# Clustered attention and an ELU product pair on one core: scores computed transposed, with the products of a batch placed beside the next batch's attention

## The chip, the core and the metric

The program runs on one core of a Trainium2 chip. Five engines have queues of their own: TensorE (PE; PEld is its weight load), VectorE (DVE), ScalarE (ACT), GpSimd (POOL) and SyncE (SP, which here issues the transfers). The metric is the device time of one execution in microseconds, median over the runs. A change of about 1% either way is taken as the least that can be told from none.

## The reference

Inputs: `q`, `k`, `v` of 4 batches x 8 heads x 768 tokens x 64, `centroids` of 8 heads x 16 x 64, all float32; `w_in` 512 x 2048 and `w_out` 2048 x 512, which arrive as float64.

```
q_assign = argmax(q_n . c_n)      k_assign = argmax(k_n . c_n)      # 16 clusters for each head
scores   = (q . k^T) / 8, and -1e9 where q_assign != k_assign
attn     = softmax over the keys (maximum subtracted first)
x        = attn . v, heads side by side: 3072 tokens x 512
h        = x @ w_in;  g = h where h > 0, else exp(h) - 1;  out = g @ w_out
```

In the reference's own arrays every one of the 4 x 8 x 16 clusters has between 26 and 72 keys (counted from them).

## The kernel before

Sixteen units of work, `pairs`: a batch and two heads. Of a pair, `turn_head` transposes q and k to 64 rows x 768 tokens with TensorE (line 183); `assign` multiplies each 128 tokens with the 16 centroids (line 200: 24 products of only 16 columns, each with a weight load of its own) and makes one-hot rows on VectorE; `clusters` transposes these (line 228) and puts them below q and k as rows 64 to 79 (`aug`), so that one product over 80 rows gives the masked score. `prepare` runs this for the next pair while a pair is in work.

A score tile is 128 queries x 768 keys of one head (`softmax`, line 254). VectorE takes the maximum (264), ScalarE the exponential and the row sum (265), VectorE the reciprocal and the product with it (268 to 270). The keys then lie along the free dimension, but the product with v sums over keys, so `turn_probs` transposes each tile in six pieces on TensorE (281), and the results are copied out of PSUM by VectorE and ScalarE in turn (`evacuate`, lines 70 and 72). `values` (292) multiplies v, 64 columns for each head: the two heads go to the upper and lower 64 partitions of one PSUM tile. When the four pairs of a batch have half their tokens done, `mlp` runs both products for these 384 tokens: 64 products into `bank` (310) with the ELU on VectorE, ScalarE, VectorE (318, 319, 321), and 48 into `o` (327). Nothing else is written beside it.

The weights are turned from float64 words to float32 in 32 pieces of 128 x 512 (`convert`): six VectorE steps (146, 148, 151, 152, 153, 158) and two of GpSimd (147, 159) each, one piece beside each score tile from the start on.

Each float32 product appears in the trace as two MATMUL instructions (`mlp` asks for 512 products at line 310; the trace has 1024); a transpose appears as one. The emitted order isn't quite that of the code: the tile framework moves instructions.

Of the kernel before, what the change touches and what calls it, by code (L numbers as in the profile page):

```python
# [11 lines left out]
U32 = mybir.dt.uint32  # L12
Act = mybir.ActivationFunctionType
# [4 lines left out]
P = 128  # L18
# Added to the score of a query and a key of different clusters. It is a power of two, so
# the products with the one-hot rows are exact, and so large that a score disappears in it:  # L20
# a query whose cluster has no key gets equal scores for all keys.
BIG = float(2.0**80)


@with_exitstack
def kernel(
# [11 lines left out]
    ctx.enter_context(nc.allow_non_contiguous_dma(reason="token and weight layouts"))  # L38

    B, H, S, D = q.shape  # L40
# [8 lines left out]
    FG = NT  # L49
    KA = D + NC  # L50
    SCALE = 1.0 / 8.0
    assert D == 64 and NC == 16 and H * NC == P and S % (2 * P) == 0 and DM == H * D

    const = ctx.enter_context(tc.tile_pool(name="const", bufs=1))
    loads = ctx.enter_context(tc.tile_pool(name="loads", bufs=2))
    work = ctx.enter_context(tc.tile_pool(name="work", bufs=3))
    small = ctx.enter_context(tc.tile_pool(name="small", bufs=4))
    augp = ctx.enter_context(tc.tile_pool(name="augp", bufs=8))
    turned = ctx.enter_context(tc.tile_pool(name="turned", bufs=5))
    xtp = ctx.enter_context(tc.tile_pool(name="xtp", bufs=10))  # L60
    ps_s = ctx.enter_context(tc.tile_pool(name="ps_s", bufs=2, space=PSUM))
    ps_t = ctx.enter_context(tc.tile_pool(name="ps_t", bufs=2, space=PSUM))
    ps_o = ctx.enter_context(tc.tile_pool(name="ps_o", bufs=2, space=PSUM))

    turn = [0]

    def evacuate(out_, in_):
        turn[0] += 1
        if turn[0] % 2:
            nc.vector.tensor_copy(out_, in_)  # L70
        else:
            nc.scalar.copy(out_, in_)  # L72

    def bank(dtype=F32):
        t = ps_t.tile([P, 512], F32, name="bank", tag="t")
        return t if dtype == F32 else t.bitcast(dtype)

# [4 lines left out]
    def load(i):  # L82
        b, pr = pairs[i]
        for name, src, bufs in (("q", q, 2), ("k", k, 2), ("v", v, 3)):
            t = loads.tile([P, 2, NT, D], F32, name=f"{name}_raw", tag=name, bufs=bufs)
            nc.sync.dma_start(
                t.rearrange("p h t d -> p h (t d)"),
                src[b, 2 * pr : 2 * pr + 2].rearrange("h (p t) d -> p h (t d)", t=NT),
            )
            raw[name, i] = t  # L90

    cen = const.tile([P, D], F32, name="cen")
    nc.scalar.dma_start(cen, centroids.rearrange("h c d -> (h c) d"))
    load(0)

    ident = const.tile([P, P], F32, name="ident")
    make_identity(nc, ident)
    identb = const.tile([P, P], BF16, name="identb")
    nc.vector.tensor_copy(identb, ident)
    rev = const.tile([P, NC], F32, name="rev")  # L100
    nc.gpsimd.iota(
        rev, pattern=[[-1, NC]], base=NC, channel_multiplier=0, allow_small_or_imprecise_dtypes=True
    )

# [4 lines left out]
    cT = const.tile([D, P], F32, name="cT")  # L109
# [3 lines left out]
    # The square root, then one step of Newton's method.  # L113
# [6 lines left out]
    nc.vector.tensor_scalar(cen, cen, norm, None, op0=Alu.mult)  # L120
    cps = bank()
    nc.tensor.transpose(cps[:D, :P], cen, ident)
    nc.vector.tensor_copy(cT, cps[:D, :P])

# [1 line left out]
    # They come as float64, as words of 64 bits, and are rounded to float32 here. With the  # L126
    # low word and the high word (sign, 11 bits of exponent, 20 of mantissa) of a number,
    #     +-2^(exponent - 1023) * ((1 + mantissa / 2^20) + low / 2^52),
    # where the last sum rounds to the nearest. What float32 cannot hold becomes 0 or
    # infinity, as its exponent is held between 0 and 255.  # L130
    w_in = const.tile([P, KC, DF], F32, name="w_in")
    w_out = const.tile([P, FC, DM], F32, name="w_out")
# [3 lines left out]
    def convert(to, src):  # L136
        """The two steps of a piece; the first makes exponent and sign, the second the number."""
# [3 lines left out]
        ex = loads.tile([P, WC], U32, name="ex", tag="ex", bufs=2)  # L141
        low, high, bits = words[:, :, 0], words[:, :, 1], to.bitcast(U32)

        def begin():
            nc.sync.dma_start(words.rearrange("p n w -> p (n w)"), src.bitcast(U32))
# [17 lines left out]
    def weights():  # L163
        for g in range(DF // WC):
            for c in range(KC):
                yield w_in[:, c, ts(g, WC)], moe_w_in[ts(c, P), ts(g, WC)]
        for f in range(FC):
            yield w_out[:, f], moe_w_out[ts(f, P)]

# [103 lines left out]
    def turn_probs(i, half, hp, t):  # L273
        p = probs.pop((i, half, hp, t))
        if t == 0:
            probsT[i, half, hp] = turned.tile([P, NT, HS], F32, name="probsT", tag="turned")
# [139 lines left out]
```

## Time and profile before

| | us |
|---|---|
| median of 3 runs | 1575.28 |
| lowest, highest | 1571.52, 1582.56 |
| the profiled execution's span | 1583.6 |
| TensorE busy in it | 1524.0 (96%) |
| VectorE, ScalarE, GpSimd busy | 788.6, 406.2, 67.6 |

The profiled execution is 0.5% above the median, within 0.1% of the slowest of the runs. Matmuls are pipelined and the ends of their intervals are modelled: neighbours overlap. So a group's mean duration is longer than the distance from one start to the next, and its busy time divided by its count is nearer to that distance.

### The profile page before, as it was taken

The numbers are of one execution on the slowest core, as the hardware profiler recorded it, in microseconds if no ns is written. First come the engines' busy times: TensorE is split into PE (matmuls) and PEld (weight loads), VectorE is DVE, ScalarE is ACT, GpSimd is POOL, SyncE is SP. The second block draws the span as 40 slices with busy tenths as digits, with TensorE's granted clock in tenths as the row PEclk, the third lists the DMA queues.
The fourth block names the chain that finished last, engine by engine and source line by source line (L and its number), as shares of the span: only waits on it lengthen the run. The fifth ranks groups of instructions, "written<-read, shape, count | busy, mean of one in ns | idle before, by whom it ended". The sixth has DMA issues, their size and how long they took to land.

```text
span 1583.6 us, 15284 instructions
## 1 busy us (share of the span) xinstructions
PE 1524.0 (96%) x6017; PEld 883.5 (56%) x6017; DVE 788.6 (50%) x1623; ACT 406.2 (26%) x831; POOL 67.6 (4%) x71
## 2 busy tenths in 40 slices
PE   6888889999999999999999999999999999999999
PEld 4645446654555666654554666565554665654453
DVE  4879796540522665741431666742340567651230
ACT  1222222310311343420311333511210335331110
POOL 1223231000000000000000000000000000000000
PEclk6667766899999898999999898999999889899999
DMA  4223130100001001100000011000000000000000
GB/s 143 74 69 121 56 121 13 31 0 14 17 0 40 8 23 31 31 0 14 17 1 20 20 31 31 30 0 7 14 11 13 27 11 1 1 0 7 14 1 20
DMA packets 21336, 42.96 MB, mean 27 GB/s; under 512 B 1808, under 2 KB 14096, under 8 KB 21264
## 3 DMA queue, kind: packets, MB, share of 16 engines
q1 hardware_dynamic: 21120, 41.95, 8.2%
q8 instruction: 47, 0.77, 0.2%
q14 instruction: 25, 0.20, 0.0%
q10 hardware_dynamic: 144, 0.03, 0.0%
HBM read 35.68 MB, written 6.29 MB: 27 GB/s over the span
## 4 chain that ended last, share of the span: by engine, by line
PE 90%; DVE 5%; ACT 3%; issue 1%; DMA 1%; SPq 0%
PE bank L310 21%; PE o L327 21%; PE scores L254 16%; PE bank L281 10%; PE o L292 10%; PE bank L200 8%; PE bank L183 2%; ACT probs L265 2%; PE bank L228 2%; DVE probs L270 1%; DVE low L264 1%; DVE ex L148 1%; ACT aug L237 1%; DMA words<-in_moe_w_in_dram 1%; DVE probsT L70 0%
## 5 line engine op out<-in xcount | busy, mean ns | idle before, releaser
L254 PE MATMUL scores<-aug 80*128 80x384 f32 x768 | 344.3, 563 | 8.3 <-ACT probs L265 6.6
L310 PE MATMUL bank<-xT,w_in 128*128 128x384 f32 x1024 | 332.4, 487 | 0.0
L327 PE MATMUL o<-w_out,gT 128*128 128x512 f32 x768 | 330.9, 592 | 0.0
L310 PEld LDWEIGHTS bank<-xT,w_in 128*128 128x128 f32 x1024 | 193.9, 190 | 138.3 <-issue 4.8
L327 PEld LDWEIGHTS o<-w_out,gT 128*128 128x128 f32 x768 | 145.9, 190 | 182.0 <-issue 177.9
L281 PEld LDWEIGHTS bank<-ident,probs 128*128 128x128 f32 x1152 | 153.6, 159 | 136.9 <-issue 49.0
L281 PE MATMUL bank<-ident,probs 128*128 128x128 f32 x1152 | 204.9, 311 | 24.5 <-ACT probsT L72 10.8
L264 DVE TENSOR_REDUCE low<-scores 128x1 f32<-128x768 f32 x192 | 182.6, 951 | 28.1 <-PE scores L254 26.0
L72 ACT COPY probsT<-bank 128x384 f32<-128x384 f32 x192 | 91.9, 479 | 397.2 <-PE bank L281 396.4
L254 PEld LDWEIGHTS scores<-aug 80*128 80x128 f32 x768 | 143.1, 216 | 81.0 <-ACT probs L265 36.6
L265 ACT ACTIVATE probs<-scores,low 128x768 f32<-128x768 f32 x192 | 173.3, 902 | 35.9 <-DVE low L264 28.9
L292 PE MATMUL o<-probsT,v_raw 128*64 128x384 f32 x768 | 175.0, 524 | 0.3 <-DVE probsT L70 0.3
L70 DVE COPY probsT<-bank 128x384 f32<-128x384 f32 x192 | 104.9, 551 | 136.0 <-PE bank L281 135.5
L319 ACT ACTIVATE elu<-elu 128x384 f32<-128x384 f32 x128 | 66.9, 523 | 296.3 <-DVE elu L318 296.3
L200 PE MATMUL bank<-cT,aug 64*128 64x16 f32 x768 | 128.5, 317 | 4.1 <-DVE aug L190 4.1
L200 PEld LDWEIGHTS bank<-cT,aug 64*128 64x128 f32 x768 | 126.8, 260 | 9.9 <-DVE aug L190 4.3
L318 DVE TENSOR_SCALAR elu<-bank 128x384 f32<-128x384 f32 x128 | 71.4, 558 | 116.9 <-PE bank L310 116.9
L270 DVE TENSOR_SCALAR probs<-probs,den 128x768 f32<-128x768 f32 x192 | 124.2, 647 | 3.5
L321 DVE SCALAR_TENSOR_TENSOR gT<-elu,bank 128x384 f32<-128x384 f32 x128 | 71.0, 554 | 82.2 <-ACT elu L319 82.2
L70 DVE COPY o_sb<-o 128x512 f32<-128x512 f32 x8 | 5.5, 692 | 205.6 <-PE o L327 205.6
L292 PEld LDWEIGHTS o<-probsT,v_raw 128*64 128x64 f32 x768 | 59.5, 144 | 74.2 <-issue 70.1
L72 ACT COPY o_sb<-o 128x512 f32<-128x512 f32 x16 | 9.4, 586 | 315.5 <-PE o L327 315.5
(55 smaller groups left out, 626.6 us busy)
## 6 DMA issues: line engine op xcount, KB each, us to landing
words<-in_moe_w_in_dram SPq DMA_DIRECT2D x16, 512.0 KB, 3.9
words<-in_moe_w_out_dram SPq DMA_DIRECT2D x16, 512.0 KB, 3.5
q_raw<-in_q_dram SPq DMA_DIRECT2D x16, 384.0 KB, 3.1
k_raw<-in_k_dram SPq DMA_DIRECT2D x16, 384.0 KB, 3.9
v_raw<-in_v_dram SPq DMA_DIRECT2D x16, 384.0 KB, 3.1
out_dram<-o_sb SPq DMA_DIRECT2D x24, 256.0 KB, 2.0
cen<-in_centroids_dram ACTq DMA_DIRECT2D x1, 32.0 KB, 2.4
```

Source lines behind the costliest of these rows:

```text
L70: nc.vector.tensor_copy(out_, in_)
L72: nc.scalar.copy(out_, in_)
L200: nc.tensor.matmul(ps[:, (2 * hp + j) * NT + t], lhsT=aug[i, hp, j][:D, ts(t, P)], rhs=cT[:, ts(h, NC)], start=True, stop=True,)
L254: nc.tensor.matmul(s[:, ch, :HS], lhsT=aug[i, hp, 0][:, ts(half * HT + t, P)], rhs=aug[i, hp, 1][:, ts(ch, HS)], start=True, stop=True,)
L264: nc.vector.tensor_reduce(low, s[:, :, :HS], axis=Axis.XY, op=Alu.max, negate=True)
L265: nc.scalar.activation(p.rearrange("p (a b) -> p a b", a=2), s[:, :, :HS], Act.Exp, bias=low, accum_out=den)
L270: nc.vector.tensor_scalar(p, p, den, None, op0=Alu.mult)
L281: nc.tensor.transpose(ps[:, ts(kt, P)], p[:, ts(g * HT + kt, P)], ident)
L292: nc.tensor.matmul(o[D * hp : D * hp + D, :HS], lhsT=raw["v", i][:, hp, kt], rhs=probsT[i, half, hp][:, kt], start=(kt == 0), stop=(kt == ...
L310: nc.tensor.matmul(h, lhsT=w_in[:, c, ts(f, P)], rhs=xT[b, half, c], start=(c == 0), stop=(c == KC - 1),)
L318: nc.vector.tensor_scalar(e, h, 0.0, None, op0=Alu.min)
L327: nc.tensor.matmul(o, lhsT=g[f // FG][:, f % FG, ts(t, P)], rhs=w_out[:, f], start=(f == 0), stop=(f == FC - 1),)
```

## The change

The program gets a main path and a general path. The main path writes into `go` whether its own sums allow its result; the general path (the arithmetic of before, in a loop over batches) runs only if they don't.

In the main path:

- **Layout.** q and k of a pair are loaded with both heads side by side and transposed as 128 x 128 tiles: `T[i, j]` has head 0 in rows 0 to 63 and head 1 in rows 64 to 127. The load's pieces are 64 numbers (256 B) where they were 384.
- **Clusters.** For a whole batch at once: `similar` multiplies the centroids as 32-column weights into four 32-partition strips of one PSUM tile; VectorE transposes in 32 x 32 blocks, compares with the maximum (`assign`), and transposes back. `count` sums the ones.
- **Scores.** A tile is 128 keys x 384 queries for both heads: two float32 products over 64 rows each, and two bf16 products over 64 rows that add 0 or -2^80 (`hot`, `qm`). ScalarE takes the exponential without a maximum. The tile is already keys by queries, so nothing is transposed and `values` reads it directly, one key tile at a time. There are again 192 tiles.
- **Denominators.** `add` sums the six tiles elementwise, on GpSimd in the first batch and on VectorE later; `divide` multiplies the sum with ones on TensorE, copies (ScalarE), takes the reciprocal of 128 x 384 (VectorE), and multiplies x on GpSimd.
- **Order.** `manual_schedule`; a batch has 48 slots of one score tile. The 56 steps of `mlp` of the batch before (4 products each) are spread over them. Batch 0's slots hold the weight conversion instead, two of its 96 steps each; a fifth round of slots has the last batch's `mlp` alone. All four pairs of a batch are turned and assigned before its first score.
- **ELU.** exp on ScalarE from PSUM, min and max on GpSimd, the last step on VectorE, issued with the step that follows.

```diff
+    main_path(tc, c, q, k, v, centroids, moe_w_in, moe_w_out, out)
+    good = nc.values_load(c["go"][0:1, 0:1], min_val=0, max_val=P)
+    with tc.If(good < P):
+        general_path(tc, c, q, k, v, out)
...
+    ctx.enter_context(tc.manual_schedule())
...
+    def similar(b, j, half):
...
+                for g in range(2):
+                    pr = 2 * g + x
+                    at = 64 * e + 32 * g
+                    nc.tensor.matmul(
+                        ps[at : at + 32, :HS],
+                        lhsT=cTz[:, pr, e].rearrange("p x c -> p (x c)"),
+                        rhs=T[b * NPR + pr, j][:, half * HS : (half + 1) * HS],
...
+    def score(i, half, kt):
...
+        for e in range(2):
+            rows = slice(64 * e, 64 * e + 64)
+            nc.tensor.matmul(
+                s[:, e, :HS],
+                lhsT=T[i, 1][rows, ts(kt, P)],
+                rhs=T[i, 0][rows, cols],
...
+        for e in range(2):
+            rows = slice(64 * e, 64 * e + 64)
+            nc.tensor.matmul(
+                s[:, e, :HS],
+                lhsT=hot[b, 1][rows, ts(kt, P)],
+                rhs=qm[i][rows, cols],
...
+        nc.scalar.activation(p, s[:, :, :HS], Act.Exp, scale=SCALE)
+
+    def add(i, half, kt, eng):
...
+        eng.tensor_tensor(
+            to, pu[i, half, 0] if kt == 1 else to, pu[i, half, kt], op=Alu.add
+        )
...
+    def divide(i, half):
...
+            nc.tensor.matmul(
+                d[64 * e : 64 * e + 64, :HS], lhsT=ones, rhs=s[:, e], start=True, stop=True
+            )
...
+        nc.scalar.activation(r, d[:, :HS], Act.Copy, accum_out=d_sum[:, n : n + 1])
+        nc.vector.reciprocal(r, r)
+        x = xT[i, half]
+        nc.gpsimd.tensor_tensor(x, x, r, op=Alu.mult)
+        nc.gpsimd.tensor_tensor(r_sum, r_sum, r, op=Alu.add)
...
+            nc.scalar.activation(t, h, Act.Exp)
+            nc.gpsimd.tensor_scalar(t, t, 1.0, 0.0, op0=Alu.min, op1=Alu.max)
...
+        for n in range(slots):
+            if b < B:
...
+                score(i, half, kt)
+                eng = nc.gpsimd if b == 0 else nc.vector
+                at(now + 1, lambda i=i, half=half, kt=kt, eng=eng: add(i, half, kt, eng))
+                at(now + LAG, lambda i=i, half=half, kt=kt: values(i, half, kt))
+                if kt == NT - 1:
+                    at(now + LAG + 1, lambda i=i, half=half: divide(i, half))
+            for step in later.pop(now, []):
+                step()
+            if b == 0:
+                weigh(2)
+            for step in plan.get(n, []):
+                step()
+            upto = (n + 1) * len(steps) // slots
+            for step in steps[done:upto]:
+                step()
...
```

## Rows read from the trace of the kernel before

**Rows 1.** The page: span, busy time by engine, granted clock in 40 slices.

```profile
span 1583.6 us, 15284 instructions
...
PE 1524.0 (96%) x6017; PEld 883.5 (56%) x6017; DVE 788.6 (50%) x1623; ACT 406.2 (26%) x831; POOL 67.6 (4%) x71
...
PEclk6667766899999898999999898999999889899999
```

**Rows 2.** Groups of TensorE by line: busy us, mean ns of one, idle before.

```profile
L254 PE MATMUL scores<-aug 80*128 80x384 f32 x768 | 344.3, 563 | 8.3 <-ACT probs L265 6.6
L310 PE MATMUL bank<-xT,w_in 128*128 128x384 f32 x1024 | 332.4, 487 | 0.0
L327 PE MATMUL o<-w_out,gT 128*128 128x512 f32 x768 | 330.9, 592 | 0.0
L281 PE MATMUL bank<-ident,probs 128*128 128x128 f32 x1152 | 204.9, 311 | 24.5 <-ACT probsT L72 10.8 <-DVE aug L190 9.4 <-ACT aug L237 1.8
...
L292 PE MATMUL o<-probsT,v_raw 128*64 128x384 f32 x768 | 175.0, 524 | 0.3 <-DVE probsT L70 0.3
...
L200 PE MATMUL bank<-cT,aug 64*128 64x16 f32 x768 | 128.5, 317 | 4.1 <-DVE aug L190 4.1
```

**Rows 3.** Two stretches: length; busy by engine (instructions); granted clock; transfers' share, GB/s.

```profile
34.70:320.00 285.30, 253.36 (x984) 151.72 (x984) 225.23 (x452) 78.40 (x160) 64.00 (x61) 0.70 0.22 69
...
1417.00:1583.00 166.00, 161.17 (x467) 82.41 (x465) 39.01 (x74) 21.47 (x42) 0.00 (x0) 1.00 0.03 10
```

**Rows 4.** TensorE in order of time, 644 to 651 us: start, length, what.

```profile
644.17 0.82 PE L281 MATMUL bank<-ident,probs 128*128 128x128 f32 x6
644.83 0.81 PE L254 MATMUL scores<-aug 80*128 80x384 f32 x2
645.48 0.86 PE L183 MATMUL bank<-ident,q_raw 128*64 128x128 f32 x6
646.27 0.87 PE L292 MATMUL o<-probsT,v_raw 128*64 128x384 f32 x4
647.07 0.84 PE L183 MATMUL bank<-ident,k_raw 128*64 128x128 f32 x6
647.84 3.44 PE L292 MATMUL o<-probsT,v_raw 128*64 128x384 f32 x18
```

**Rows 5.** TensorE in order of time, 312 to 317 us.

```profile
312.44 0.84 PE L228 MATMUL bank<-identb,oh 128*16 128x128 bf16 x12
313.21 4.08 PE L292 MATMUL o<-probsT,v_raw 128*64 128x384 f32 x22
```

**Rows 6.** VectorE and GpSimd in order of time, 36.5 to 38.7 us.

```profile
36.54 1.37 POOL L159 TENSOR_TENSOR w_in<-w_in,ex 128x512 f32<-128x512 f32 x1 [6.32 <-DVE w_in L158]
36.71 1.49 DVE L148 TENSOR_SCALAR ex<-words 128x512 uint32<-128x512 uint32 x1
...
38.00 0.68 POOL L147 TENSOR_SCALAR w_in<-w_in 128x512 f32<-128x512 uint32 x1
```

**Rows 7.** Groups of the other engines by line.

```profile
L265 ACT ACTIVATE probs<-scores,low 128x768 f32<-128x768 f32 x192 | 173.3, 902 | 35.9 <-DVE low L264 28.9 <-DVE den L269 5.5 <-DVE den L268 0.7
...
L321 DVE SCALAR_TENSOR_TENSOR gT<-elu,bank 128x384 f32<-128x384 f32 x128 | 71.0, 554 | 82.2 <-ACT elu L319 82.2
...
L148 DVE TENSOR_SCALAR ex<-words 128x512 uint32<-128x512 uint32 x32 | 33.0, 1031 | 0.0
...
L159 POOL TENSOR_TENSOR w_in<-w_in,ex 128x512 f32<-128x512 f32 x16 | 22.5, 1405 | 91.7 <-DVE w_in L158 57.2 <-DVE ex L153 19.4 <-DVE den L268 15.1
...
L152 DVE TENSOR_SCALAR ex<-ex 128x512 uint32<-128x512 uint32 x32 | 13.3, 416 | 0.1
...
L158 DVE SCALAR_TENSOR_TENSOR w_in<-words,w_in 128x512 f32<-128x512 uint32 x16 | 10.9, 681 | 0.0
```

**Rows 8.** All engines in order of time: the first scores.

```profile
34.71 5.49 PE L254 MATMUL scores<-aug 80*128 80x384 f32 x8
```

**Rows 9.** All engines in order of time: the last transfer's issue.

```profile
1580.65 0.33 SPq L336 DMA_DIRECT2D out_dram<-o_sb  x1
```

## Prediction on record before the run

> **What bounds the kernel now.** I read the page's busy times first. TensorE has work in 1524.0 of 1583.6 us, the other engines in half of it or less [rows 1]. So the time is TensorE's work at its clock, and a change pays by taking work from TensorE or by letting its clock rise. The grouped lines say where that work lies [rows 2]: scores 344 us, transposes of the probabilities 205, values 175, the centroid products 128, and 663 for the two products of `mlp` (332 + 331). The stretches say at which clock: while the weights are converted beside batch 0, TensorE is granted 0.70 of full speed, so a mixture of the levels 1.2 and 2.4 GHz, and is not always busy; in the last stretch, only products, it is at 1.00 [rows 3].
>
> **Unit costs at full clock.** A MATMUL of 384 columns costs 332.4 / 1024 = 0.325 us, and a float32 product takes two: 0.65. Six transposes take 0.66 from start to start (644.17 to 644.83), 0.11 each. The rows of `values` show how the new scores may go: its two heads use different 64 columns of the array, and 18 instructions take 3.44 us, 0.19 each and not 0.325; they run two at a time [rows 4], as 22 in 4.08 us do [rows 5]. A pair alone, with the turn to this layout and back, takes 0.80 (646.27 to 647.07), and the six transposes around it 0.79 and 0.77 where they otherwise take 0.66. So a pair costs 0.65 and each change between layouts 0.11 to 0.15; I take 0.13. A bf16 instruction of 128 columns takes 0.77 / 12 = 0.064 [rows 5], so one of 384 columns 0.17 to 0.19: 0.18.
>
> **What goes from TensorE.** The 1152 transposes (205 us), the centroid products (128), and their copies and reductions on VectorE and ScalarE, which had no part in the bound. `values` keeps its 384 products. `mlp` keeps all of its own.
>
> **What a score tile costs now.** Two float32 products, one on the upper and one on the lower 64 rows of the array, writing to two banks, then two bf16 ones. Whether row halves run side by side no row shows; the nearest is the column halves of [rows 4]. Bounds: 0.65 + 0.18 = 0.83 side by side, 1.30 + 0.36 = 1.66 one after the other (before: 344.3 / 192 = 1.79 with its clock). I take 0.83, as in the rows of column halves. The Trainium skill, TensorE: Matmul & The Clock Gate, Part 3 (Packing small matmuls), says that products in distinct row groups run concurrently and gives 3.07 times for four of 32 rows; by it the sum would be the one I take, but no row here shows it for rows.
>
> **A slot of batches 1 to 3.** Score 0.83, values 0.65, three layout changes (rows, columns, full) 0.39: 1.87 us; 48 of them 89.8. Besides, per batch: `divide` 8 x 0.65 = 5.2 (two column halves of ones), turns 48 x 0.11 = 5.3, `similar` 4 calls x 2 rounds x 0.65 = 5.2 if its four strips run together (20.8 if not), and `mlp` 663.3 / 4 = 165.8. Sum 271.3; batch 3 prepares none, 260.8. Three rounds: 803. The fifth round is products alone: 166.
>
> What hides the rest in these rounds: a slot lasts 271 / 48 = 5.6 us. ScalarE has one exponential of 768 (0.90), two thirds of one of 384 and a few copies, some 1.6; VectorE an addition of 768 (about 1.5 times the 0.554 of 384, 0.9) and two thirds of a 0.554 step; GpSimd two thirds of a tensor-scalar of 384 (0.75 x 0.68 = 0.5) [rows 6, 7]. All is below half of the slot, so I cost it at nothing. Without that cover (a stall of TensorE on `bank`, which has two buffers and waits for exp, min/max and the VectorE step, about 1.7 us against the 1.5 of score and values that stand between), it is a few tenths for some of the 56 steps: under 10 us a batch. The reciprocal of 384 has no row: at least 0.55 (the VectorE step of 384), at most 1.05 by the slowest elementwise row (1.40 x 384 / 512 = 1.05) [rows 7]. Eight a batch, hidden in both cases.
>
> **Batch 0.** Nothing of `mlp` is there, but 27 of the 32 weight pieces are (five go with the preparation). TensorE's own work: 48 x (0.83 + 0.65 + 0.26) + 5.2 + 5.3 + 5.2 = 99 us at full clock, some 195 at 1.2 GHz. GpSimd gets the additions: a tensor-tensor of 512 takes 1.40 [rows 7], so of 768 2.11; 40 of them 84 us. With two of 384 in each `divide` (16 x 1.05 = 17) and 27 pieces x (1.40 + 0.68) = 56 it has 157 us [rows 6, 7]. VectorE has four plain steps of 0.416 and two of 0.68 a piece, 3.03 x 27 = 82 us [rows 7], and about 25 more.
>
> Do these two run side by side? In [rows 6] VectorE's L148 starts 0.17 us behind GpSimd's L159 and takes 1.49 us where its neighbour L152 takes 0.416 [rows 7]: it ends 0.29 us after L159 does. Over the kernel L148 has a mean of 1.03 [rows 7]: 0.6 us lost, each time. So one waits for the other. For the steps with two inputs (L153, L158, the additions) no row shows an overlap. Bounds: 157 us if these don't exclude each other, 157 + 82 = 239 if all do. I take 239, by the L148 rows, and 1 for the waits in which neither works: GpSimd stands at `divide` until TensorE, ScalarE and VectorE have answered, but then VectorE has weight steps to do. So 240, more than TensorE's 195. TensorE feels it at once: its queue is in order, `divide` needs the sum, and the additions hold `p`, of which there are six. Low end 195 (TensorE at 1.2 GHz with a loose pair), high end 275. The Trainium skill, VectorE: DVE Perf Modes (section Walkthrough: the 8-slice pipeline in each mode), has a reciprocal repeat its divide step 8 times; as an estimate from that page's 0.96 GHz, 3.2 us for 384 elements, for which GpSimd would wait in each `divide`: up to 8 x 3.2 = 26 us more and a sum of 1288. No row here shows it. The Trainium skill, SBUF — State Buffer, section SBUF: two separate sides, says that VectorE instructions in a two-port mode, or with two SBUF inputs against a GpSimd one that reads SBUF, and GpSimd's exclude each other for the whole instruction. By it the batch takes the 239 and not 157; the L148 rows agree for the first kind, no row here shows the second.
>
> **Start and end.** The first scores stand at 34.7 us before [rows 8], for one pair. Now four pairs are turned (two raw buffers, so the loads of pairs 2 and 3 wait for turns), four `similar`, two `assign`, and five weight pieces lie in VectorE's queue: 5 x 3 us and some 20 more. I take 45 us, between 35 and 65. The end: the last transfer is issued 2.95 us before the end now [rows 9]; the check's reductions are done long before, but its product, a copy, a register load and a branch stand behind the last copy: I take 8 us, 4 to 15.
>
> **Sum.** 45 + 240 + 803 + 166 + 8 = 1262, against 1583.6 of the profiled execution, whose runs have a median of 1575.28, 0.5% less. That difference is within the bounds, so I say 1260 us.
>
> **Rivals.**
> - *The row halves don't run side by side.* For it: rows show only columns. Against: the array splits by columns without loss. In three rounds 144 x 0.83 = 120 us more; in batch 0 TensorE at 1.2 GHz has 195 + 80 = 275 instead of 240. 1262 + 120 + 35 = 1417.
> - *Batch 0 is TensorE's.* GpSimd's additions and VectorE's steps pass each other. 195 instead of 240: 1217; with more of the full clock as low as 170: 1190.
> - *The clock falls beside the products (slower).* In the rounds 1 to 3 half-array products alternate with full ones, with a layout change every other microsecond. If a share w of that work runs at 1.2 GHz, the rounds take 803 x (1 + w): 1575 is passed from w = 0.39 on, and w = 1 gives 2065. For it: the 0.70 while batch 0 was in work, with TensorE busy in 253 of 285 us. Against: 3.5 of a slot's 5.6 us are the products that have 1.00 [rows 3], and nothing makes TensorE wait.
> - *The check sends it into the general path*, which is before's arithmetic in a loop: at least 1262 + 1575 = 2840. One query whose cluster has no key (an infinite reciprocal) or one tie decides it. The reference's smallest cluster has 26 keys, so only a tie can.
>
> **Chances.** The forecast 0.66, with a range of its own from 1215 to 1310; a cheaper batch 0 0.12; row halves in sequence 0.14; the clock 0.05; the general path 0.02; the rest 0.01. The range reaches from the cheap batch 0 with a short start, 1170, to the row halves in sequence, 1425: it leaves out the two slower cases and half of the third. Faster by over 1% (about what a measurement of this kernel can tell from no change) 0.93, within 1% 0.01, slower 0.06.
>
> **What would show it.** Row halves: the starts of the two float32 products of `score` lie together, and the six instructions of a tile take about 0.83 us. Batch 0: GpSimd busy nearly throughout, VectorE's weight steps at twice their length or more, clock near 0.5. Rounds 1 to 3: about 270 us each, clock 1.00, TensorE without idle time. No instruction of the general path after `go`. The prediction is wrong in its main term if TensorE idles in rounds 1 to 3, or if a layout change between row and column halves costs much more than 0.13.

## The result, and the profile of the changed kernel

The changed kernel takes 1280.4 us (median of 4 runs, 1279.5 to 1282.6) against 1578.9 for the kernel before on the same chip: 0.811 of its time, interval 0.809 to 0.814. The forecast was 1260, its own range 1215 to 1310. The profiled execution's span is 1278.8.

First the page: busy times by engine, then VectorE's busy tenths and the granted clock in 40 slices.

```profile
PE 1132.8 (89%) x4291; PEld 486.1 (38%) x4291; DVE 494.5 (39%) x596; ACT 281.8 (22%) x475; POOL 296.7 (23%) x303
...
DVE  5888888833321335223321335223322332220110
...
PEclk9877777899999999999999999999999999999999
```

Against [rows 1], TensorE's busy time fell by 391 us and the span by 305. VectorE is at 8 tenths in the seven slices of batch 0 that have the lowered clock, and at 1 to 3 after that; from there on the clock is full.

The stages, by the first scores of each round and the last instructions: length; busy us (instructions) of TensorE, its weight load, VectorE, ScalarE, GpSimd; granted clock; transfers' share, GB/s.

```profile
35.50:258.50 223.00, 118.81 (x616) 41.81 (x612) 187.54 (x210) 49.40 (x77) 138.78 (x107) 0.76 0.29 85
258.50:547.10 288.60, 280.67 (x1074) 118.77 (x1072) 92.03 (x104) 69.22 (x118) 49.16 (x53) 1.00 0.08 21
547.10:835.80 288.70, 280.62 (x1073) 118.76 (x1072) 92.01 (x104) 69.59 (x118) 40.77 (x48) 1.00 0.06 17
835.80:1272.60 436.80, 435.07 (x1422) 197.53 (x1422) 100.56 (x123) 86.44 (x151) 60.21 (x82) 1.00 0.03 10
1272.60:1278.75 6.15, 0.17 (x3) 0.07 (x2) 0.15 (x1) 0.59 (x1) 0.00 (x0) 0.82 0.15 55
```

| stage | forecast | measured | difference |
|---|---|---|---|
| start and batch 0 | 45 + 240 = 285 | 35.5 + 223.0 = 258.5 | -26.5 |
| round 1 | 271.3 | 288.6 | +17.3 |
| round 2 | 271.3 | 288.7 | +17.4 |
| round 3 and the last products | 260.8 + 166 = 426.8 | 436.8 | +10.0 |
| end | 8 | 6.2 | -1.8 |
| sum | 1262.4 | 1278.8 | +16.4 |

The sum is 1.3% off because errors of both signs lie in it: start and batch 0 were 10% too long, rounds 1 and 2 6% too short. The rest of this document is about these differences.

A slot of round 2, TensorE in order of time: start, length, what.

```profile
706.69 0.92 PE L311 MATMUL scores<-qT,kT 64*128 64x384 f32 x4
707.44 0.33 PE L320 MATMUL scores<-qm,hot 64*128 64x384 bf16 x2
707.70 0.87 PE L345 MATMUL o<-p,v_raw 128*64 128x384 f32 x4
708.49 2.85 PE L383 MATMUL bank<-xT,w_in 128*128 128x384 f32 x8
711.27 0.92 PE L311 MATMUL scores<-qT,kT 64*128 64x384 f32 x4
```

From start to start: the two float32 score products 0.75 us, the mask pair 0.26, `values` 0.79, four products of the batch before (eight instructions) 2.78. The score pair is four instructions of 384 columns on different row halves in 0.75 us; one after the other they would take 4 x 0.325 = 1.30.

Batch 0 around the end of a row of six additions: what each engine runs, and in brackets what it stood for.

```profile
129.16 1.37 POOL L198 TENSOR_TENSOR w_out<-w_out,ex 128x512 f32<-128x512 f32 x1 [2.15 <-DVE w_out L197]
130.50 1.80 POOL L336 TENSOR_TENSOR psum<-psum,p 128x768 f32<-128x768 f32 x1
130.57 2.01 DVE L187 TENSOR_SCALAR ex<-words 128x512 uint32<-128x512 uint32 x1 [1.15 <-POOL w_out L198]
...
132.35 1.55 PE L360 MATMUL bank<-psum,ones 128*64 128x384 f32 x4 [13.98 <-POOL psum L336]
...
135.21 1.43 POOL L198 TENSOR_TENSOR w_out<-w_out,ex 128x512 f32<-128x512 f32 x1 [2.16 <-DVE w_out L197]
135.43 2.55 DVE L366 RECIPROCAL r<-r 128x384 f32<-128x384 f32 x1
```

VectorE's L187 (the old L148) first waits 1.15 us for GpSimd's L198, because `ex` has one buffer; then it starts 0.07 us behind a GpSimd addition and ends 0.28 us after it. TensorE stands 13.98 us at `divide` for the sum. Between 45 and 235 us its waits of this kind are 48.9 us for VectorE, whose queue holds a copy that has to free a buffer, and 40.6 for GpSimd's additions: us in total, times, longest.

```profile
PE bank L360 <- DVE kT L236: 48.9, 3, 16.8
PE bank L360 <- POOL psum L336: 40.6, 3, 14.8
```

Two groups of VectorE: busy us, mean ns of one, idle before and its releaser. The reciprocal takes 2.55 us, and L187 takes almost four times the 0.416 of its neighbour in [rows 7].

```profile
L366 DVE RECIPROCAL r<-r 128x384 f32<-128x384 f32 x32 | 81.7, 2552 | 216.5 <-ACT r L365 216.5
...
L187 DVE TENSOR_SCALAR ex<-words 128x512 uint32<-128x512 uint32 x32 | 50.2, 1567 | 21.9 <-POOL w_out L198 11.5 <-POOL w_in L198 10.4
```

The stage's first line, 35.50, is where the first float32 score products stand, and these need no mask. The first mask product comes 9 us later:

```profile
44.60 0.50 PE L320 MATMUL scores<-qm,hot 64*128 64x384 bf16 x2 [8.17 <-DVE qm L278]
```

So the preparation of batch 0 ends at 44.6 us, as forecast (45), and batch 0 from there takes 213.9 us, where 240 were forecast.

### The profile page after: what moved, and what is told of

The parts are those of the page before. It is cut to its first block, busy times and chain, and to the rows that moved or that the text cites. A ratio compares the mean times of both kernels' runs of the same rounds, so it can differ in the third digit from the quotient of the medians.

```text
span 1278.8 us, 10641 instructions
## 1 busy us (share of the span) xinstructions
PE 1132.8 (89%) x4291; PEld 486.1 (38%) x4291; DVE 494.5 (39%) x596; ACT 281.8 (22%) x475; POOL 296.7 (23%) x303
## 4 chain that ended last, share of the span: by engine, by line
PE 78%; POOL 8%; DVE 7%; issue 4%; ACT 2%; SPq 1%; DMA 0%; ACTq 0%; POOLq 0%
PE f L413 25%; PE bank L383 24%; PE scores L311 10%; PE o L345 8%; POOL psum L336 4%; PE h L383 3%; PE o L413 2%; PE scores L320 2%; DVE r L366 1%; PE bank L360 1%; PE bank L247 1%; DVE ex L187 1%; PE bank L231 1%; DVE kT L236 1%; POOL w_out L198 1%
## 5 line engine op out<-in xcount | busy, mean ns | idle before, releaser
L413 PE MATMUL f<-w_out,gT 128*128 128x512 f32 x704 | 320.4, 602 | 4.1 <-ACT o_sb L422 4.1
L328 ACT ACTIVATE p<-scores 128x768 f32<-128x768 f32 x192 | 155.8, 812 | 370.5 <-PE scores L320 363.1
L413 PEld LDWEIGHTS f<-w_out,gT 128*128 128x128 f32 x704 | 128.3, 190 | 181.5 <-issue 171.9
L393 POOL TENSOR_SCALAR gT<-gT 128x384 f32<-128x384 f32 x128 | 64.8, 506 | 528.4 <-ACT gT L392 528.4
L311 PE MATMUL scores<-qT,kT 64*128 64x384 f32 x768 | 179.6, 545 | 0.0
L345 PE MATMUL o<-p,v_raw 128*64 128x384 f32 x768 | 170.0, 522 | 0.0
L366 DVE RECIPROCAL r<-r 128x384 f32<-128x384 f32 x32 | 81.7, 2552 | 216.5 <-ACT r L365 216.5
L398 DVE SCALAR_TENSOR_TENSOR gT<-gT,bank 128x384 f32<-128x384 f32 x112 | 61.7, 551 | 260.6 <-POOL gT L393 260.6
L336 DVE TENSOR_TENSOR psum<-psum,p 128x768 f32<-128x768 f32 x96 | 105.3, 1097 | 91.8 <-ACT p L328 91.4
L360 PE MATMUL bank<-psum,ones 128*64 128x384 f32 x128 | 31.8, 579 | 91.1 <-DVE kT L236 48.9
L320 PE MATMUL scores<-qm,hot 64*128 64x384 bf16 x384 | 64.0, 326 | 8.2 <-DVE qm L278 8.2
L187 DVE TENSOR_SCALAR ex<-words 128x512 uint32<-128x512 uint32 x32 | 50.2, 1567 | 21.9 <-POOL w_out L198 11.5
```

What stands on the lines that cost most here:

```text
L187: nc.vector.tensor_scalar(ex, high, 20, 0x7FF, op0=Alu.logical_shift_right, op1=Alu.bitwise_and)
L311: nc.tensor.matmul(s[:, e, :HS], lhsT=T[i, 1][rows, ts(kt, P)], rhs=T[i, 0][rows, cols], start=True, stop=False,)
L320: nc.tensor.matmul(s[:, e, :HS], lhsT=hot[b, 1][rows, ts(kt, P)], rhs=qm[i][rows, cols], start=False, stop=True,)
L328: nc.scalar.activation(p, s[:, :, :HS], Act.Exp, scale=SCALE)
L336: eng.tensor_tensor(to, pu[i, half, 0] if kt == 1 else to, pu[i, half, kt], op=Alu.add)
L345: nc.tensor.matmul(o[64 * e : 64 * e + 64, :HS], lhsT=raw["v", i][:, e, kt], rhs=pu[i, half, kt][:, e], start=(kt == 0), stop=(kt == NT - 1),)
```

## Do the row halves run side by side?

Theory: the two heads' score products share the array, so a tile costs half of what it would in sequence. The rival is that the saving has another source (no transposes, fewer weight loads) and the row halves hardly matter. Two kernels bear on it. The first orders the four products so that those of one half follow each other:

```diff
         for e in range(2):
             ... float32 product of head e
-        for e in range(2):
-            rows = slice(64 * e, 64 * e + 64)
             ... mask product of head e, now right behind it
```

> The four products of a score tile in the order float32 head 0, mask head 0, float32 head 1, mask head 1, so that the two float32 products no longer stand next to each other; nothing else changes. If the upper and lower 64 rows work side by side only for products that follow each other: a tile goes from 1.01 us (0.75 + 0.26 in the changed kernel's trace) to about 0.75 + 0.65 + 0.26 = 1.6 us, 0.6 us x 144 tiles in the three rounds with products = 86 us more, and little in batch 0, where TensorE waits 93 us anyway: 1360 to 1380 us. If the array runs one product after the other whatever the order, or keeps both going in any order: 1280 us, as before the edit.

Measured: 1282.4 us, ratio 0.812 (0.809 to 0.815), rounds of 288.8 and 288.9: no change. That is the second outcome that was expected, and it has two readings (one after the other whatever the order, or both at once whatever the order). The trace says which one. The program's order on TensorE was head 0, its mask, head 1, its mask; the slot in time reads:

```profile
707.14 0.92 PE L311 MATMUL scores<-qT,kT 64*128 64x384 f32 x4
707.89 0.33 PE L318 MATMUL scores<-qm,hot 64*128 64x384 bf16 x2
```

All four float32 instructions still stand together, 0.75 us ahead of the mask pair; the first one of each half starts at 707.141 and 707.151. The second head's product ran before a mask product that was issued ahead of it. So this order doesn't part the halves, and the run's time tells nothing between theory and rival. The second kernel puts all four on rows 0 to 63 (it computes head 0's scores twice):

```diff
-            rows = slice(64 * e, 64 * e + 64)
+            rows = slice(0, 64)
```

> All four products of a score tile read rows 0 to 63, so the second head's scores are those of the first (this part of the computation is changed); their number, columns and order stay. Theory, row halves run side by side (starts 7 ns apart in the changed kernel): without it a tile takes 1.30 + 0.36 = 1.66 us instead of 1.01, and 144 tiles of the rounds with products give 94 us more; batch 0 takes little more, as TensorE waits 93 us in it: total 1375 to 1395 us. Rival, the 64-row products are short for another reason and the halves do not matter: 1280.

Measured: 1420.1 us, ratio 0.900 (0.898 to 0.902). Rounds 1 and 2 take 327.1 and 327.2, 38.5 us more each, which is 48 x 0.80; batch 0 takes 248.2, 25 more. The time is above the 1375 to 1395 expected, because a tile costs 0.80 more and not 0.65, and because batch 0 was expected to stay: TensorE, busy 118.8 of its 223.0 us in the changed kernel, is busy 236.8 of 248.2 here. A slot:

```profile
810.84 1.55 PE L311 MATMUL scores<-qT,kT 64*128 64x384 f32 x4
812.23 0.48 PE L320 MATMUL scores<-qm,hot 64*128 64x384 bf16 x2
812.65 0.87 PE L345 MATMUL o<-p,v_raw 128*64 128x384 f32 x4
```

The pair takes 1.39 us where it took 0.75, the mask pair 0.42 where it took 0.26. The row halves are worth 140 us of the whole. Each tile costs 0.80 more, where the prediction's bounds were 0.83 apart. The prediction's rival, halves one after the other, came to 1417, and 1420.1 lies close to it by luck: it had 155 us more (120 + 35) on a sum that was itself 18 us below what was measured.

## What sets the time of batch 0?

The prediction put batch 0 at the sum of GpSimd's and VectorE's work, because they hold each other. The rivals: one engine alone decides (GpSimd with its additions, or VectorE with the weights). Three kernels move work in three ways, and one takes a wait away.

**Additions of batch 0 on VectorE.**

```diff
-                eng = nc.gpsimd if b == 0 else nc.vector
+                eng = nc.vector
```

> The 40 elementwise additions of batch 0 go from GpSimd (1.80 us each when nothing holds them) to VectorE (0.90). Theory, the two engines exclude each other, batch 0 lasts the sum of both (217 us from the first masked scores): the sum falls by 40 x 0.90 = 36 us, total near 1245. Rival, VectorE alone sets batch 0: 36 us more, near 1316. Rival, GpSimd alone: it falls from 146 to 74 us, and the batch ends at what VectorE has of its own, some 170: near 1232.

Measured: 1261.1 us, ratio 0.799 (0.797 to 0.801), batch 0 201.3 instead of 223.0. VectorE got more to do and the batch became shorter, so it isn't VectorE's own work alone; but it is 21.7 us and not the 36 expected of mutual exclusion. In batch 0 VectorE's busy time is nearly what it was (189.0 us against 187.5) though 38.5 us of additions are in it, so it is held some 37 us less; and its wait for GpSimd's L198 fell from 21.9 us to 1.2.

**Part of the weights later**: one step a slot in batch 0, three in each of the first twelve slots of round 1, so that 11 pieces move.

```diff
-                weigh(2)
+                weigh(1)
+            if b == 1 and n < 12:
+                weigh(3)
...
-            if b == 1:
-                weigh(2)
```

> Eleven of the 27 weight pieces of batch 0 (all of them of the second product) go to the first 12 slots of the next round, three steps a slot. Exclusion theory: each piece is 2.08 us of GpSimd and 3.03 us of VectorE, so batch 0 gets 11 x 5.1 = 56 us shorter (217 to about 160), and the next round hides most of it (12 slots are 70 us, both engines need some 75 in them): 288 to 290 to 300. Total 1230 to 1240. Rival, GpSimd alone: 23 us less in batch 0; rival, VectorE alone: 33 us less; total 1250 to 1260 in both.

Measured: 1266.1 us, ratio 0.802 (0.800 to 0.804). Batch 0 takes 174.4, 48.6 less; of the theories only the mutual exclusion (56) is near. But round 1 takes 321.8, 33 more, so that the total is above all that were expected. In that round TensorE's products wait for VectorE, whose queue holds the weight steps ahead of what they need. TensorE's waits in that round: us in total, times, longest.

```profile
PE bank L231 <- DVE kT L236: 15.7, 4, 13.7
PE bank L383 <- DVE gT L398: 10.6, 3, 4.0
```

**GpSimd's two steps of a weight piece on VectorE.**

```diff
-            nc.gpsimd.tensor_scalar(to, bits, 2.0**-20, 1.0, op0=Alu.mult, op1=Alu.add)
+            nc.vector.tensor_scalar(to, bits, 2.0**-20, 1.0, op0=Alu.mult, op1=Alu.add)
...
-            nc.gpsimd.tensor_tensor(to, to, ex.bitcast(F32), op=Alu.mult)
+            nc.vector.tensor_tensor(to, to, ex.bitcast(F32), op=Alu.mult)
```

> The two GpSimd steps of each weight piece (0.68 and 1.27 us unheld) go to VectorE (about 0.42 and 0.68). Exclusion theory: 27 pieces x (1.95 - 1.10) = 23 us less in batch 0, total near 1257. Rival, VectorE alone sets batch 0: 30 us more, near 1310. Rival, GpSimd alone: it falls from 146 to 91 us, and the batch ends at VectorE's own, then some 170: near 1232.

Measured: 1282.6 us, ratio 0.812 (0.810 to 0.815), batch 0 221.7: nothing gained, and none of the three expectations met. This decides against the plain sum. Both engines' work together is less, yet the time stays. GpSimd's waits between 45 and 235 us (us in total, times, longest) and a stretch in which it adds without a pause, with VectorE's weight steps beside it:

```profile
POOL xT L368 <- DVE r L366: 104.9, 6, 18.4
```

```profile
144.53 8.23 POOL L336 TENSOR_TENSOR psum<-psum,p 128x768 f32<-128x768 f32 x4
...
146.72 2.18 DVE L192 SCALAR_TENSOR_TENSOR ex<-words,ex 128x512 uint32<-128x512 uint32 x1
...
148.82 2.29 DVE L197 SCALAR_TENSOR_TENSOR w_out<-words,w_out 128x512 f32<-128x512 uint32 x1
```

GpSimd stood 104.9 us at `divide` for the reciprocal, where in the changed kernel the same wait between 45 and 235 us is 16.5: the reciprocal stands in VectorE's queue behind the weight steps, and each of these takes as long as a GpSimd addition. So both things are there: the engines hold each other (0.7 us becomes 2.2 for steps with two inputs), and VectorE's queue is in order, with GpSimd empty while it waits for an answer out of it. The sum holds only where the other engine always has something to do.

**A second buffer for `ex`** (room from one buffer less for `o_sb`) takes away the 21.9 us that VectorE's L187 waits for GpSimd's L198:

```diff
-        ex = loads.tile([P, WC], U32, name="ex", tag="ex", bufs=1)
+        ex = loads.tile([P, WC], U32, name="ex", tag="ex", bufs=2)
...
-                o_sb = work.tile([P, DM], F32, name="o_sb", tag="o_sb")
+                o_sb = work.tile([P, DM], F32, name="o_sb", tag="o_sb", bufs=1)
```

> The changed kernel with two buffers for ex instead of one (and one instead of two for o_sb, to make room), so that VectorE's L187 no longer waits for GpSimd's L198 of the piece before (21.9 us of waits in batch 0). Theory, the two engines exclude each other: L187 then stands behind the same L198 as a held instruction, and batch 0 stays at 223 us within 6: total 1274 to 1281. Rival, it is a plain wait in VectorE's queue: 20 us less, near 1260.

Measured: 1276.0 us, ratio 0.808 (0.805 to 0.812), batch 0 218.1. The wait is gone, but the next step takes longer instead; the same groups of this kernel:

```profile
L190 DVE TENSOR_SCALAR ex<-ex 128x512 uint32<-128x512 uint32 x32 | 45.6, 1425 | 1.1
...
L187 DVE TENSOR_SCALAR ex<-words 128x512 uint32<-128x512 uint32 x32 | 42.2, 1320 | 0.0
```

L190 went from a mean of 0.79 us to 1.43. That is 20 us more in all, while L187 lost 8. Of 21.9 us of wait 4.9 came back as time (two kernels with the same batch 0 differ by 3: 223.0 in the changed kernel and 225.9 in the one with one block below); the rest was turned into being held by GpSimd, for VectorE's busy time rose by 16.8 us (187.5 to 204.3). That is what mutual exclusion says and a mere lack of a buffer doesn't.

Taken together: batch 0 lasts as long as VectorE's queue, its own steps and what GpSimd holds it for. In the changed kernel VectorE is busy, held or not, 187.5 us of 223.0, stands 21.9 at L187 for GpSimd and 7.9 at the reciprocal for ScalarE's copy: 217.3. The same count gives 198.1 of 201.4 us with the additions on VectorE, 169.0 of 174.4 with part of the weights later, 214.1 of 221.7 with GpSimd's steps on VectorE and 212.2 of 218.1 with two buffers: 97 to 98% in all five, while GpSimd's busy time lies between 38 and 65% of the stage.

## Where do 17 us a round come from?

Theory: the layout changes of TensorE's array and waits on `bank`, both from the products being spread over the slots. The rival is that the products or the scores themselves cost more than forecast, wherever they stand. The first kernel puts all 56 product steps of a batch into one block behind its fourth slot:

```diff
-            upto = (n + 1) * len(steps) // slots
+            upto = (n + 1) * len(steps) // slots if b == B else len(steps) * (n >= 3)
```

> The 56 steps of the products of a batch stand in one block behind the fourth slot of the next round instead of being spread over 48 slots. Theory, TensorE's time in the rounds is the sum of its instructions and its layout changes: 44 slots have two changes instead of three (0.17 us each: 416 ns to the next start instead of 323, and a longer first pass) and no buffer of bank is waited for between scores: 8 to 15 us less a round, total 1235 to 1256. Rival, the spreading is what keeps the clock at 1.00 and hides exponential and additions: the attention slots alone are granted 0.5 to 0.9 or wait for ScalarE and VectorE, 10 to 90 us more a round, total above 1310.

Measured: 1245.7 us, ratio 0.789 (0.788 to 0.791), 35 us less. Round 1 (round 2 takes 273.1), and 80 us with attention alone:

```profile
262.60:536.10 273.50, 270.43 (x1074) 122.47 (x1072) 93.32 (x101) 70.12 (x119) 47.96 (x52) 1.00 0.09 24
450.00:530.00 80.00, 80.00 (x490) 29.09 (x490) 61.20 (x56) 38.61 (x61) 19.55 (x12) 1.00 0.18 45
```

A round is 15.4 us shorter: TensorE's busy time fell by 10.3 with the same instructions, and its idle time from 8.0 to about 3. So the products cost no more in themselves; their places do. The attention alone keeps TensorE busy without a gap and at full clock, so nothing needs the products as a filling.

The second kernel keeps the spreading but handles two tiles together (scores, scores, values, values, then the products of two slots), which halves the layout changes:

```diff
-        for n in range(slots):
-            if b < B:
-                ...
+        for first in range(0, slots, 2):
+            for n in (first, first + 1):
+                if b < B:
+                    ...
+            for m in (now - 2, now - 1):
+                for step in later.pop(m, []):
+                    step()
+            for n in (first, first + 1):
+                ... the product steps of both slots
```

> Two slots are merged: two score tiles, then the values of two tiles, then the steps of both slots. Theory, a change of layout costs 0.17 us: half of 3 x 144 go, 72 x 3 x 0.17 = 37 us less, total near 1245; batch 0, which waits for GpSimd and VectorE, stays at 223. Rival, the changes are cheap and the 17 us a round above the forecast are waits on bank: the same or, with three or four steps in a row on two buffers, up to 10 us a round more: 1275 to 1310.

Measured: 1283.3 us, ratio 0.813 (0.810 to 0.815), rounds 287.5 and 288.9: no gain, as the rival had it. The changes are fewer, but four times a round a block of eight products (16 instructions) waits in its middle for a buffer of `bank` to be read out. TensorE and then VectorE in order of time, and TensorE's waits between 550 and 830 us:

```profile
703.36 2.85 PE L383 MATMUL bank<-xT,w_in 128*128 128x384 f32 x8
708.40 2.85 PE L383 MATMUL bank<-xT,w_in 128*128 128x384 f32 x8 [2.19 <-DVE gT L398]
```

```profile
702.86 2.55 DVE L366 RECIPROCAL r<-r 128x384 f32<-128x384 f32 x1 [5.77 <-ACT r L365]
705.33 0.89 DVE L336 TENSOR_TENSOR psum<-p 128x768 f32<-128x768 f32 x1
706.26 1.62 DVE L336 TENSOR_TENSOR psum<-psum,p 128x768 f32<-128x768 f32 x1
707.80 0.54 DVE L398 SCALAR_TENSOR_TENSOR gT<-gT,bank 128x384 f32<-128x384 f32 x1
```

```profile
PE bank L383 <- DVE gT L398: 8.8, 4, 2.2
```

In round 2 TensorE's busy time fell from 280.6 to 271.0 us, and its idle time rose from 8.1 to 17.8: what the layout changes gave, these waits took. The VectorE step that frees the buffer was ready (GpSimd's min/max before it ended at 700.64), but it is issued with the step that follows, and so it stands in VectorE's queue behind the reciprocal of a `divide` and two additions. All four waits of round 2 come behind one of its eight `divide`s. That is read from the trace; no run issues the step earlier. In the kernel with one block no `divide` lies within the block, and no wait for L398 is in its round 2.

## What the parts give together

The block and the additions on VectorE, both edits as above:

> The products of a batch in one block behind the fourth slot, and the additions of batch 0 on VectorE. The first touches only the rounds (35 us less alone), the second only batch 0 (19 us less alone), so they should add up: 1280.4 - 35 - 19 = 1226 us. If they share a cause (the first rounds' waits on VectorE), less: 1235 to 1245.

Measured: 1222.7 us, ratio 0.774 (0.771 to 0.777); batch 0 200.9, rounds 273.1: the two gains add up. The block and seven weight pieces moved beside it (steps 1 or 2 a slot in batch 0, the rest in round 1):

```diff
-                weigh(2)
+                weigh(1 if n % 4 else 2)
+            if b == 1 and n < 3:
+                weigh(1)
...
+            for x, step in enumerate(steps[done:upto]):
+                if b == 1 and x < FC:
+                    weigh(2 if x < 2 else 1)
+                if b == 1 and x == FC:
+                    weigh(1000)
```

> The products in one block, and 7 of the 27 weight pieces of batch 0 moved beside the first 16 steps of that block and the three slots ahead of it, where VectorE has 1.7 us of weight work for each 2.6 us of TensorE. Theory, batch 0 is VectorE's own work plus the time GpSimd holds it: 4.4 us less for each piece (48.6 us for 11 pieces before), 31 us less in batch 0, and nothing added to the round as VectorE is nearly idle in the block: 1245.7 - 31 = 1215. Rival, what is moved comes back in the round (33 of 49 us did when three steps a slot were put between scores): 1235 to 1245.

Measured: 1220.5 us, ratio 0.773 (0.770 to 0.776); batch 0 45.7 us shorter, round 1 20.5 us longer than with the block alone. So the total is near the 1215 of the theory, but not by its way: it had 31 and nothing. All three edits:

> All three edits: one block, additions of batch 0 on VectorE, 7 weight pieces beside the block. Theory: 1245.7 - 31 - 19 = 1196, or a little more, because with less work in batch 0 TensorE's own 100 to 195 us at its mixed clock begin to show: 1195 to 1210. Rival, the additions on VectorE weigh more once GpSimd holds it less: no gain over the kernel with the block and the weights alone, 1215.

Measured: 1199.8 us, ratio 0.759 (0.756 to 0.762). Batch 0 there:

```profile
36.30:200.30 164.00, 115.47 (x616) 41.32 (x612) 149.08 (x194) 49.41 (x77) 66.56 (x54) 0.84 0.33 93
```

GpSimd's busy time is halved. VectorE, with 36 additions more (39 us) but seven weight pieces less (7 x 3.03 = 21 us), is busy 149.1 us against 187.5: it is held less. At last the loop over two tiles, as above, on top of that:

> The kernel with one block, additions of batch 0 on VectorE and 7 weight pieces beside the block, and besides two score tiles, then the values of two, in the attention slots. If the merged slots failed to gain beside spread products only because four steps in a row waited for bank (the block has its waits anyway, the attention slots use bank rarely): 48 changes of layout less a round at 0.17 to 0.23 us, 8 to 11 us a round, three rounds: 1199.8 - 24 to 33, 1167 to 1176. Rival, a change of layout costs nothing that anything else would not fill (the two score buffers, waits for the exponential): 1195 to 1205.

Measured: 1186.6 us, ratio 0.751 (0.748 to 0.754), the best of these kernels and 7.3% below the changed one. It gives 13 us where 24 to 33 were expected. Two tiles on TensorE, and one single tile in the attention stretch of the kernel with one block:

```profile
701.66 0.92 PE L311 MATMUL scores<-qT,kT 64*128 64x384 f32 x4
702.41 0.33 PE L320 MATMUL scores<-qm,hot 64*128 64x384 bf16 x2
702.58 0.81 PE L311 MATMUL scores<-qT,kT 64*128 64x384 f32 x4
703.22 0.33 PE L320 MATMUL scores<-qm,hot 64*128 64x384 bf16 x2
703.48 1.51 PE L345 MATMUL o<-p,v_raw 128*64 128x384 f32 x8
704.92 0.87 PE L231 MATMUL bank<-ident,q_raw 128*128 128x128 f32 x6
```

```profile
453.20 0.92 PE L311 MATMUL scores<-qT,kT 64*128 64x384 f32 x4
...
455.00 0.92 PE L311 MATMUL scores<-qT,kT 64*128 64x384 f32 x4
```

Two tiles take 3.26 us (701.66 to 704.92) where two single ones take 2 x 1.80 = 3.60 (453.20 to 455.00): two layout changes less, 0.17 each. A part of that is seen at one place: the mask pair takes 0.17 between two score pairs (702.41 to 702.58) and 0.26 ahead of `values` (703.22 to 703.48). Over 24 double tiles that is 8 us a round, and TensorE's busy time in round 2 did fall by 7.8 (270.3 to 262.5); but its idle time rose by 4.9, by waits for a mask (1.5 us), for a sum that `divide` needs (1.4), for the VectorE step of the ELU (1.1) and for a turn's copies (1.0), so that 2.8 are left of it.

## Why the prediction was right, and where it wasn't

**Transposes, centroid products and `values`.** As forecast: the transposes of the probabilities are gone with nothing in their place on TensorE, the centroid products have shrunk to `similar`, 5.7 us a round from start to start (5.2 forecast, 128 / 4 = 32 before), and `values` reads the score tiles as they are.

**Row halves.** Right, and now shown: 0.75 + 0.26 with the layout changes in it, against 1.39 + 0.42 on the same rows. The Trainium skill, TensorE: Matmul & The Clock Gate, Part 3 (Packing small matmuls), says that products in distinct row groups run concurrently; the trace agrees.

**The clock.** That rival fell: 1.00 in every round, also in the stretch of attention alone, as in the last stretch of before [rows 3]. Only batch 0, where TensorE stands for others, has 0.76, a mixture of 1.2 and 2.4 GHz; the prediction's sign for it was near 0.5. The general path didn't run: behind `mlp`'s last product TensorE has only the one that adds up the sums.

**Start.** Right: the first mask product stands at 44.6 us, against the 45 forecast. The 35.5 of the table is only the first float32 scores, behind which TensorE stands 8.2 us for the masks. So what the table's first line is too long by lies in batch 0.

**Batch 0.** 213.9 from the first mask on (223.0 in the table) and not 240. The step that failed is the sum of both engines' work. The addition takes 1.87 us on the mean and not 2.11, and 36 of the 40 fall into the stage: 67 us where 84 stood, so GpSimd is busy 138.8 and not 157. With that, the prediction's own sum is 138.8 + 28 x 3.03 = 224 for the 223.0, but that is luck. The sum leaves out VectorE's other steps, 39 us in this stage; GpSimd, which was to be busy nearly throughout, is idle for 84 us of it; and with GpSimd's weight steps on VectorE the sum would be some 23 us less, where nothing was gained. That the engines hold each other is right; what sets the time is VectorE's queue with what it is held for, 97 to 98% of the stage in five kernels. The reciprocal takes 2.55 us, far outside of my bounds of 0.55 to 1.05: a row of another operation bounds nothing for one that divides. The Trainium skill, VectorE: DVE Perf Modes (Walkthrough: the 8-slice pipeline in each mode), led to an estimate of 3.2 us; the measurement decides, 2.55, but the page was nearer than the rows. In batch 0 GpSimd waits 16.5 us in six `divide`s until it is done. The Trainium skill, SBUF — State Buffer, section SBUF: two separate sides, has a GpSimd instruction that reads SBUF exclude VectorE's two-input steps too; the rows of 2.18 and 2.29 us in the kernel with GpSimd's weight steps on VectorE agree.

**Rounds 1 to 3.** Two steps failed: the slot's price, and a wait left out of the sum. A slot takes 1.98 us of attention (0.75 + 0.26 + 0.79, and 2.78 - 8 x 0.325 = 0.18 that the products lose behind it) against 1.46 of work without a layout change (0.65 for the scores, 0.16 for the masks, 0.65 for `values`): 0.52 for three changes, 0.17 each and not 0.13. That is 48 x 0.11 = 5.3 us of the 17. TensorE is idle 8.0 us a round. I had bounded a wait on `bank` by 10 us a batch and costed it at nothing, but the chain that I named for it (exp, min/max, VectorE step) is in none of these waits. TensorE's waits in round 1:

```profile
PE bank L231 <- DVE kT L236: 2.6, 4, 0.7
PE bank L383 <- DVE kT L236: 2.6, 4, 0.7
PE f L413 <- ACT o_sb L422: 1.4, 2, 0.7
```

With 1.0 more for the copy of q, 6.2 us of them are turns, and products behind turns, that wait until the copy of a turn has left its buffer of `bank`; in the kernel with one block, where the products stand apart from the turns, these waits are gone. The remaining 4 us lie in TensorE's busy time. By the starts in the trace, eight turns of six transposes take 7.9 us of round 2 without their waits, where 5.3 stood: 2.6 of the 4; `similar`, `divide` and the products are 0.4 to 0.5 above their terms each. What I never asked is whether spreading the products pays at all: the block behind the fourth slot is 35 us faster, so this part of the change is a loss beside the simpler order.

**Last products and end.** 10.0 and 1.8 off. Round 3 has the layout changes of the others, but no turns and so none of their waits. The end, 6.2 us, is within its bounds of 4 to 15; the check's reductions were done by 1234.4 us, as the prediction had it.

So the forecast's mechanism held for TensorE (what goes, the row halves, the clock) and not for the time of batch 0. That its total was 1.6% off is in part luck: a batch 0 and an end that were 28.3 us too long stood against rounds that were 44.7 too short.

## What to carry to other kernels

When two engines exclude each other, don't add their work: follow the queue that others wait on, with the time it is held, and move off the *other* engine what holds it; a buffer more only turns waiting into being held. On TensorE count the changes of array layout like instructions, and before spreading one stage's products over another's slots, ask what gap they are to fill: here there was none, and one block was 35 us better. A wait that is bounded by 10 us a round belongs in the sum with its middle, not with nothing; and ask of a buffer who else uses it: here the copies of the turns held `bank`, not the chain that was named. Look, too, at what stands ahead in an engine's queue: a step that is issued late can wait behind a reciprocal though its input is ready.

## What was new about the hardware

- TensorE doesn't keep the issue order between row halves: with the order head 0, mask 0, head 1, mask 1, the second head's float32 product started 10 ns after the first, ahead of the mask product issued before it. The Trainium skill, TensorE: Matmul & The Clock Gate, Part 3, has MATMULs start and end in program order; this trace differs, and the measurement decides.
- A change of array layout (rows, columns, full) costs about 0.17 us at full clock: 0.52 us for the three of a slot, and 0.34 less where two tiles handled together have two changes fewer. What fills this time no run here shows.
- A reciprocal of 128 x 384 float32 takes 2.55 us on VectorE, on the mean of 32, and ran beside a GpSimd step without either growing by more than 0.1 us.
- A VectorE step with two inputs in SBUF, 0.68 us by itself, took 2.18 to 2.29 beside back-to-back GpSimd additions. It goes the other way too: in the kernel with the additions on VectorE, a GpSimd step that takes 1.37 us in the rows above took 1.91, begun 0.16 us behind a VectorE addition; the mean of that step rose from 1.35 to 1.65. The two in order of time:

```profile
133.21 0.95 DVE L336 TENSOR_TENSOR psum<-psum,p 128x768 f32<-128x768 f32 x1
...
133.37 1.91 POOL L198 TENSOR_TENSOR w_out<-w_out,ex 128x512 f32<-128x512 f32 x1 [2.15 <-DVE w_out L197]
```
